# Moving the splitting steps of the next four heads within the attention loop

## The chip, the cores and the metric

The kernel runs on one core of a Trainium2 chip. The metric is the time of one execution on the device in microseconds (us). Three runs of the kernel before took 743.78, 744.02 and 741.24 us, with a median of 743.78 us. The engines are TensorE (PE for its matmuls, PEld for its weight loads), VectorE (DVE), ScalarE (ACT), GpSimd (POOL) and SyncE (SP), which only issues transfers here.

## The reference

An attention in which a query sees only the keys of its own cluster is followed by a mixture of experts: a token goes to one group out of four and in it to one expert out of four.

```python
def _attn_ref(q, k, v, centroids):          # q, k, v: 4 x 8 x 768 x 64
    q_assign = argmax(einsum('bhsd,hcd->bhsc', q_n, c_n), -1)    # 16 clusters a head
    k_assign = argmax(einsum('bhsd,hcd->bhsc', k_n, c_n), -1)
    mask = q_assign[:, :, :, None] == k_assign[:, :, None, :]
    scores = where(mask, scale * matmul(q, k.transpose(0, 1, 3, 2)), -1e9)
    scores = scores - max(scores, -1)
    attn = exp(scores)
    attn = attn / (sum(attn, -1) + 1e-09)
    return matmul(attn, v)
def _moe_ref(x, w_group, w_expert, w1, w2):  # x: 3072 x 512
    ...                                      # group and expert by argmax, softmax weights
    h = maximum(xg[mask_e] @ w1[g, e], 0.0)  # 512 x 1024
    out[tok_idx] = combined[:, None] * (h @ w2[g, e])
```

## The kernel before, in words

The 32 heads of the four batches are worked through one after the other, and each head in nine **units** of 512 columns, so that there are 288 units, numbered g. In each unit TensorE computes a fine score tile `psf` (L421 and L422, from two fp16 halves of each number), a coarse score tile `psc` for a head two heads further on (L379, 18 units ahead), and adds the products with the values of the unit five back to `pso` (L447, L448). ScalarE takes the exponential of `psf` (L426), GpSimd forms the low half of the result (L428), and VectorE takes the row maximum of `psc` (L382). After nine units VectorE and ScalarE divide and store the head's output (`finish`, L461 to L468).

Beside this, the inputs of the heads to come are prepared, four heads (two pairs, p0 and p1) at a time. A group of four heads is called Q and its own units begin at g = 36 Q, so that the preparation has a **cycle of 36 units**; a unit's place in it, g modulo 36, is its phase. The preparation has nine steps, whose units stand in the list `pos`:

- `split` (L199 and `halves`, L223 and L224): the fp16 high half of the keys or queries of a pair is made on ScalarE (L199), and the low half in two pieces, in the step's unit and the next: ScalarE copies half of the input to a `psm` tile (L223) and VectorE subtracts (L224).
- `assign` (L268 to L280): 36 small matmuls give the similarity to the centroids in a `psm` tile, and VectorE turns it into one-hot rows in six instructions (L273, L275, L276, L278, twice L280). Then `spread` sends the halves to their places by transfers on SP.
- `mask` (L336 to L344): the one-hot rows of four heads are transposed, scaled and sent to the score operands. The coarse scores of the group can begin after that, 18 units before its own first unit.
- `splitv` (L249, L223, L224): the same split for the values of a pair, which are needed only five units after the first unit of the pair.

`psm` tiles lie in two PSUM banks that all of these steps share with the transposes of the row maximum (L403), of the routing logits of a finished pair of heads (`logits`, L765 to L779) and of the routing decision of a finished batch (`decide`, L845 to L926). The helper `beside(g)` runs in each unit what `at` has put there, and then at most one of the waiting `turns` (assign, mask, row maximum, logits, routing); a unit in which `halves` took a `psm` tile lets no turn in, and a turn with a lower priority number goes first. A list scheduler then puts each engine's instructions in order and may draw an instruction ahead where its inputs are there: the high half of the values (L249), which needs no `psm` tile, is done some 18 units before the low half.

When the third batch is decided, `first` prepares the first expert beside the last units: it picks the expert, loads and splits its weights (L1042 to L1051), gathers its tokens (L1193) and transposes them to `xTA` (L1208, L1209). After the last unit come the logits and the decision of the last batch, which give the order of the experts (`ei`, L1347) and with it the stream of weights, and beside them the first expert's up-projection (L1236).

The lines that place the nine steps are, for Q from 2 to 7:

```python
g0 = max(0, 9 * (4 * Q - 5) + 1)                       # 36 Q - 44
g1 = 9 * (4 * Q - 2) - 9 if Q > 1 else 15              # 36 Q - 27
pos = [int(g0 + (g1 - g0) * i / (n - 1)) for i in range(n)] if Q > 1 else [...]
at(pos[0], *hold, split, p0, 0); at(pos[1], *hold, split, p0, 1)
at(pos[2], turn, pos[2], assign(p0)); at(max(pos[2], free), spread, p0)
at(pos[6], *((splitv, p0) if Q > 1 else (later, splitv, p0)))
at(pos[8], turn, pos[8], mask(Q))
```

Of the kernel before, what the change touches and what calls it, by code (L numbers as in the profile page):

```python
# [34 lines left out]
def attention(ctx, tc, qT, kT, vr, cen, R, DEN, cfg):  # L35
# [438 lines left out]
    def at(g, f, *a):  # L474
        jobs.setdefault(int(g), []).append((f, a))
# [31 lines left out]

    for Q in range(1, NQ):
        g0 = max(0, 9 * (4 * Q - 5) + 1)
        g1 = 9 * (4 * Q - 2) - 9 if Q > 1 else 15  # L510
        n = 9
        p0, p1 = 2 * Q, 2 * Q + 1
        pos = [int(g0 + (g1 - g0) * i / (n - 1)) for i in range(n)] if Q > 1 else [0, 1, 6, 3, 4, 9, 20, 23, 12]
        hold = (later,) if Q == 2 else ()
        free = max(9 * (4 * Q - 4), 0)
        if Q > 1:
            at(g0 - 4, load, p0)
            at(g0 - 4, loadv, p0)
            at(pos[0], *hold, split, p0, 0)
            at(pos[1], *hold, split, p0, 1)  # L520
        if Q > 1:
            at(pos[0], *((behind, load) if Q == 2 else (load,)), p1)
        at(*((pos[0], loadv) if Q > 1 else (16, behind, loadv)), p1)
        at(pos[2], turn, pos[2], assign(p0))
        at(max(pos[2], free), spread, p0)
        hold = (later,) if Q == 1 else ()
        at(pos[3], *hold, split, p1, 0, Q == 1)
        at(pos[4], *hold, split, p1, 1, Q == 1)
        at(pos[5], turn, pos[5], assign(p1))
        at(max(pos[5], free), spread, p1)  # L530
        at(pos[6], *((splitv, p0) if Q > 1 else (later, splitv, p0)))
        at(pos[7], *((splitv, p1) if Q > 1 else (later, splitv, p1)))
        at(pos[8], turn, pos[8], mask(Q))
# [78 lines left out]
    g, n = 0, AHEAD0  # L612
# [1000 lines left out]
def tile_cluster_attention_moe(ctx, tc, qT, kT, vr, cen, wr, w1, w2, out):  # L1613
# [25 lines left out]
    with ExitStack() as c:  # L1639
        attention(c, tc, qT, kT, vr, cen, R, DEN, cfg)  # L1640
# [58 lines left out]
```

## Time and profile before

| | value |
|---|---|
| median of three runs | 743.78 us |
| the profiled execution, its own time | 742.52 us |
| its span, first to last instruction | 740.7 us |
| PE busy (matmuls) / PEld busy (weight loads) | 720.3 us (97%) / 619.1 us (84%) |
| DVE / ACT / POOL busy | 596.1 / 486.0 / 493.6 us |
| granted TensorE clock, mean of the span | 0.997 |
| units of the attention | about 24 to 402 us of the span |
| experts | about 402 to 740 us of the span |

Busy times are sums over one engine, and engines run beside one another, so that they don't add up to the span. A matmul row is about 0.19 us long, though the next one of the same kind can start 0.03 us later; the matmul row of a short wait can therefore hide part of it. In tables by stretch each engine has its busy time and, in brackets, its number of instructions. "Idle before" in a group is time in which the group's engine had nothing to run just ahead of it, and what ended it stands behind the arrow. The chain of waits goes back from the last instruction and names at each step the work that released the next; a stretch in which the chain stays on one engine is paced by that engine.

### The profile page before, as it was taken

Reading aid. Unit: us, or ns where it says so; the run is one execution under the profiler, and the core shown is the slowest. Engines: PE = TensorE matmul, PEld = TensorE weight load, DVE = VectorE, ACT = ScalarE, POOL = GpSimd, SP = SyncE. Lnnn points to the kernel's source line nnn. Section 1 sums busy time; section 2 is a strip of 40 time slices with the busy share of each in tenths; the row PEclk is TensorE's granted clock in tenths of the full one; section 3 lists DMA queues with packets and bytes.
Section 4 is the critical chain, followed back from the end, with each engine's and each line's share of the span. In section 5 each row is a group of like instructions: output and inputs, shape, how many; then the busy total and the mean of one; then the engine's idle time right before and its main releaser. Section 6 shows DMA issues by size and latency. Waiting matters only on the chain.

```text
span 740.7 us, 26722 instructions
## 1 busy us (share of the span) xinstructions
PE 720.3 (97%) x11106; PEld 619.1 (84%) x11106; DVE 596.1 (80%) x1216; ACT 486.0 (66%) x952; POOL 493.6 (67%) x491
## 2 busy tenths in 40 slices
PE   8899999999999999999999989999999999999996
PEld 4688788888888888888888677888789999999996
DVE  6899889899888997989876476767779889988961
ACT  7778877788778887677977275444454555555642
POOL 8899787777787877878786325354644688554542
PEclk9999999999999999999999999999999999999998
DMA  8955634435245351240521696866777678887921
GB/s 226 224 141 153 192 100 119 155 99 154 81 120 172 95 159 37 67 131 3 178 81 38 234 313 220 273 211 221 237 244 234 230 272 284 284 275 264 281 77 36
DMA packets 45881, 128.04 MB, mean 173 GB/s; under 512 B 7699, under 2 KB 12691, under 8 KB 45752
## 3 DMA queue, kind: packets, MB, share of 16 engines
q1 hardware_dynamic: 40668, 112.64, 49.8%
q0 software_dynamic: 4928, 13.59, 5.1%
q8 instruction: 89, 1.46, 0.8%
q14 instruction: 40, 0.33, 0.1%
q10 hardware_dynamic: 156, 0.03, 0.0%
HBM read 93.41 MB, written 13.65 MB: 145 GB/s over the span
## 4 chain that ended last, share of the span: by engine, by line
PE 67%; DVE 17%; ACT 6%; issue 5%; DMA 2%; POOL 1%; another core or an unknown queue 1%; POOLq 0%; ACTq 0%; DVEq 0%
PE psh L1236 16%; PE psy L1258 12%; DVE mpart L382 7%; PE pso L447 6%; PE psf L421 6%; PE pso L448 5%; PE psf L422 5%; PE psc L379 5%; PE psy L1272 3%; DVE parts L224 2%; ACT p L426 2%; DMA st<-w 2%; PE psm L765 2%; PE psm L1294 1%; PE psm L1208 1%
## 5 line engine op out<-in xcount | busy, mean ns | idle before, releaser
L428 POOL TENSOR_TENSOR pl<-p 128x512 f16<-128x512 f32 x278 | 285.4, 1042 | 75.1 <-ACT p L426 70.6
L382 DVE TENSOR_REDUCE mpart<-psc 128x1 f32<-128x512 f32 (+1 forms) x282 | 190.2, 682 | 28.8 <-PE psc L379 28.4
L426 ACT ACTIVATE p<-psf 128x512 f32<-128x512 f32 x288 | 169.7, 596 | 45.6 <-PE psf L422 40.4
L447 PE MATMUL pso<-V,p 128*128 128x65 f16 x1152 | 160.2, 193 | 0.0
L448 PE MATMUL pso<-V,pl 128*128 128x64 f16 x1152 | 159.9, 193 | 0.0
L447 PE MATMUL pso<-V,pl 128*128 128x65 f16 x1152 | 159.4, 193 | 0.5 <-POOL pl L428 0.5
L448 PE MATMUL pso<-V,p 128*128 128x64 f16 x1152 | 159.3, 193 | 0.0
L421 PE MATMUL psf<-A 82*128 82x384 f16 (+2 forms) x576 | 142.5, 273 | 1.7 <-ACT p L426 1.6
L422 PE MATMUL psf<-B 128*128 128x384 f16 (+2 forms) x576 | 142.7, 273 | 0.0
L448 PEld LDWEIGHTS <-p 128*128 128x128 bf16 x1152 | 112.2, 97 | 22.2
L447 PEld LDWEIGHTS <-p 128*128 128x128 bf16 x1152 | 113.1, 98 | 9.6 <-issue 1.6
L447 PEld LDWEIGHTS <-pl 128*128 128x128 f16 x1152 | 112.5, 98 | 0.6 <-POOL pl L428 0.6
L448 PEld LDWEIGHTS <-pl 128*128 128x128 f16 x1152 | 111.5, 97 | 0.3
L379 PE MATMUL psc<-A 80*128 80x512 f16 (+1 forms) x376 | 106.3, 325 | 1.9 <-DVE mpart L382 1.2
L1239 DVE SCALAR_TENSOR_TENSOR hl<-psh,hh 128x160 f16<-128x160 f32 (+14 forms) x136 | 49.8, 368 | 48.9 <-ACT hh L1238 43.5
L1238 ACT ACTIVATE hh<-psh 128x160 f16<-128x160 f32 (+14 forms) x136 | 45.8, 345 | 59.1 <-PE psh L1236 54.9
L1301 POOL DMA_INDIRECT out_dram<-y,ri x33 | 43.4, 1316 | 52.4 <-ACT y L1300 46.3
L1236 PE MATMUL psh<-xT,wh0a 128*128 128x288 f16 (+7 forms) x512 | 74.6, 255 | 0.0
L1193 POOL DMA_INDIRECT xg<-xbuf,ri x25 | 40.5, 1620 | 43.7 <-PE psm L1208 30.1
L422 PEld LDWEIGHTS <-B 128*128 128x128 f16 x576 | 56.5, 98 | 10.9 <-issue 2.3
L1236 PE MATMUL psh<-xT,wh0b 128*128 128x272 f16 (+6 forms) x448 | 64.7, 253 | 0.0
L1236 PE MATMUL psh<-xT,wl0a 128*128 128x288 f16 (+7 forms) x256 | 64.0, 255 | 0.0
(385 smaller groups left out, 1785.9 us busy)
## 6 DMA issues: line engine op xcount, KB each, us to landing
st<-w SPq DMA_DIRECT2D x128, 512.0 KB
B<-parts SPq DMA_DIRECT2D x60, 192.0 KB
kx<-kT SPq DMA_DIRECT2D x16, 384.0 KB
qx<-qT SPq DMA_DIRECT2D x16, 384.0 KB
vx<-vr SPq DMA_DIRECT2D x16, 384.0 KB
xbuf<-xs SPq DMA_DIRECT2D x4, 1536.0 KB
A<-parts SPq DMA_DIRECT2D x30, 192.0 KB
A<-mk SPq DMA_DIRECT2D x56, 24.0 KB
```

Source lines behind the costliest of these rows:

```text
L379: last["mm"] = nc.tensor.matmul(out=pc[:, off:off + k1 - k0], lhsT=QA[h % 8][0:80, c * P:(c + 1) * P], rhs=KA[h % 8][0:80, k0:k1], start=T ...
L382: nc.vector.tensor_reduce(out=(mp[:, 0, 0:1], mp[:, :, 1], mp[:, 1, 0:1])[i], in_=pc.rearrange("p (a x) -> p a x", a=n), axis=AX.X, op=ALU ...
L421: nc.tensor.matmul(out=o, lhsT=KA[h % 8][0:82, ks], rhs=QA[h % 8][0:82, q0:q1], start=True, stop=False)
L422: nc.tensor.matmul(out=o, lhsT=KBs[h][:, ks], rhs=QBs[h][:, q0:q1], start=False, stop=True)
L426: cfg["exp"] = nc.scalar.activation(out=p32, in_=pf, func=AF.Exp, scale=QK / (SQ * SQ))
L428: lo = (nc.vector if u in (EARLY if h < 2 else DVE_LO[h % 8] if h < NH - 2 else DVE_END) else nc.gpsimd).tensor_tensor(out=pl, in0=p32, in ...
L447: nc.tensor.matmul(out=O[:, col:col + 65], lhsT=p[:, bs], rhs=vh, start=c == 0 and q == 0 and i == 0, stop=False, skip_group_check=True)
L448: nc.tensor.matmul(out=O[:, col:col + 64], lhsT=p[:, bs], rhs=vl, start=False, stop=c == NCH - 1 and i == 1, skip_group_check=True)
L1236: self.mm = nc.tensor.matmul(out=ph[:, 0:M], lhsT=w[:, k, fs], rhs=xT[:, a, k], start=i == 0, stop=i == 3 * KD - 1)
L1238: nc.scalar.activation(out=hh[:, f], in_=ph[:, 0:M], func=AF.Relu)
L1239: self.ev = nc.vector.scalar_tensor_tensor(out=hl[:, f], in0=ph[:, 0:M], scalar=0.0, in1=hh[:, f], op0=ALU.max, op1=ALU.subtract)
L1258: self.mm = nc.tensor.matmul(out=py[:, 0:M], lhsT=w[:, f, d * P:(d + 1) * P], rhs=a[:, f], start=i == 0, stop=i == len(prods) - 1)
```

## The change

Only the units of the nine steps change, for the groups Q = 2 to 7. Written as the number of units ahead of the group's first unit:

| step | before | after |
|---|---|---|
| split p0, keys or queries | 44 and 42 | 44 and 41 |
| assign p0 | 40 | 38 |
| split p1 | 38 and 36 | 36 and 33 |
| assign p1 | 34 | 31 |
| values p0, values p1 | 32 and 30 | 24 and 20 |
| mask | 27 | 27 |

The four splits of keys and queries, which followed one another two units apart, now mostly have three units each, and the values go behind the mask, to phases 12 and 16. The loads of the inputs and the `spread` of p0 keep their units; the `spread` of p1 moves by three.

```diff
     for Q in range(1, NQ):
         g0 = max(0, 9 * (4 * Q - 5) + 1)
-        g1 = 9 * (4 * Q - 2) - 9 if Q > 1 else 15
-        n = 9
         p0, p1 = 2 * Q, 2 * Q + 1
-        pos = [int(g0 + (g1 - g0) * i / (n - 1)) for i in range(n)] if Q > 1 else [0, 1, 6, 3, 4, 9, 20, 23, 12]
+        pos = [36 * Q - x for x in (44, 41, 38, 36, 33, 31, 24, 20, 27)] if Q > 1 else [0, 1, 6, 3, 4, 9, 20, 23, 12]
```

Line numbers behind this place are two lower in the changed kernel.

On VectorE, in the cycle of the group Q = 4, the values of p0 (`V_192`) stand in the block of the preparation before, between the row maxima (L382), the second pair's one-hot rows (L273 to L276) and the end of a head (L461 to L466):

```order
L382 TENSOR_REDUCE mpart_220<-psc 128x1 x2
L224 TENSOR_TENSOR V_192<-psm,V_192 128x6x64
L273 TENSOR_REDUCE mx<-psm 128x24
L224 TENSOR_TENSOR V_192<-psm,V_192 128x6x64
L382 TENSOR_REDUCE mpart_220<-psc 128x2
L461 TENSOR_SCALAR DEN<-pso 128x6
L275 TENSOR_TENSOR psm<-psm,mx 128x384
L463 RECIPROCAL rec<-DEN 128x6
L382 TENSOR_REDUCE mpart_220<-psc 128x1
L466 TENSOR_TENSOR pso<-pso,rec 128x6x64
L276 TENSOR_TENSOR psm<-psm,desc 128x384
```

In the changed kernel the values of both pairs stand behind the block:

```order
L382 TENSOR_REDUCE mpart_218<-psc 128x1
L224 TENSOR_TENSOR V_192<-psm,V_192 128x6x64
L382 TENSOR_REDUCE mpart_218<-psc 128x1
L224 TENSOR_TENSOR V_192<-psm,V_192 128x6x64
L382 TENSOR_REDUCE mpart_218<-psc 128x2
L461 TENSOR_SCALAR DEN<-pso 128x6
L463 RECIPROCAL rec<-DEN 128x6
L466 TENSOR_TENSOR pso<-pso,rec 128x6x64
L382 TENSOR_REDUCE mpart_218<-psc 128x1
L468 TENSOR_TENSOR xs<-pso,xs 128x6x64
L224 TENSOR_TENSOR V_193<-psm,V_193 128x6x64
L382 TENSOR_REDUCE mpart_218<-psc 128x1
```

The four value halves (L224) have moved from among the one-hot rows to a place where the row maxima and the end of a head alone stand beside them.

On ScalarE, around the start of a head (phases 35 to 3), in the cycle of Q = 4 as well, the kernel before has, between the exponentials (L426):

```order
L426 ACTIVATE p_4616<-psf 128x512
L199 ACTIVATE parts<-kx 128x768
L426 ACTIVATE p_4647<-psf 128x512
L426 ACTIVATE p_4690<-psf 128x512
L390 ACTIVATE desc<-m_4670 128x6
L223 ACTIVATE psm<-kx 128x384
L426 ACTIVATE p_4722<-psf 128x512
L406 COPY mr<-psm 6x128
L426 ACTIVATE p_4760<-psf 128x512
L223 ACTIVATE psm<-vx 128x384 x2
```

and the changed kernel:

```order
L426 ACTIVATE p_4612<-psf 128x512
L923 COPY rls<-psm 64x289
L390 ACTIVATE desc<-m_4678 128x6
L426 ACTIVATE p_4655<-psf 128x512
L199 ACTIVATE parts<-qx 128x768
L199 ACTIVATE parts<-kx 128x768
L223 ACTIVATE psm<-qx 128x384
L426 ACTIVATE p_4702<-psf 128x512
L223 ACTIVATE psm<-qx 128x384
L426 ACTIVATE p_4734<-psf 128x512
L406 COPY mr<-psm 6x128
L223 ACTIVATE psm<-kx 128x384
```

The second pair's two high halves (L199) and its first low half now follow one another between two exponentials, and the values' halves (`vx`) are gone from here.

On VectorE at the end of the attention, behind GpSimd's last work that VectorE does for it (L428), the kernel before has the copies of the first expert's transposed tokens (`xTA`) beside the end of the last head (L461 to L468):

```order
L428 TENSOR_TENSOR pl<-p_11278 128x512
L1209 COPY xTA<-psm 128x8x128
L779 TENSOR_TENSOR lg<-psm,lg 128x60
L1209 COPY xTA<-psm 128x8x128
L461 TENSOR_SCALAR DEN<-pso 128x6
L1209 COPY xTA<-psm 128x8x32
L463 RECIPROCAL rec<-DEN 128x6
L466 TENSOR_TENSOR pso<-pso,rec 128x6x64
```

and the changed kernel:

```order
L428 TENSOR_TENSOR pl<-p_11276 128x512
L777 TENSOR_TENSOR lg<-psm,lg 128x60
L1049 TENSOR_TENSOR wl1a<-psm,wh1a 128x2x256
L1207 COPY xTA<-psm 128x8x128
L461 TENSOR_SCALAR DEN<-pso 128x6
L463 RECIPROCAL rec<-DEN 128x6
L466 TENSOR_TENSOR pso<-pso,rec 128x6x64
L1207 COPY xTA<-psm 128x8x128
L468 TENSOR_TENSOR xs<-pso,xs 128x6x64
L1207 COPY xTA<-psm 128x8x32
L1250 MEMSET yh 128x48
L1250 MEMSET yl 128x48
```

The preparation of the first expert has moved some units back: a half of its weights (`wl1a`) and all three copies of `xTA` now stand among the last head's instructions, and the second large copy is ahead of the last head's low half (`xs`).

## Rows read from the trace of the kernel before

**Rows 1.** Busy us by engine (instructions), clock, DMA in each stretch of the span.
```profile
core 0: us, PE busy (x) PEld busy (x) DVE busy (x) ACT busy (x) POOL busy (x), PEclk, DMA share, GB/s
60.00:96.00 36.00, 34.44 (x674) 28.58 (x671) 30.01 (x66) 30.35 (x61) 29.23 (x38) 1.00 0.57 156
96.00:132.00 36.00, 36.00 (x712) 30.05 (x711) 32.27 (x70) 27.77 (x58) 30.21 (x45) 1.00 0.42 118
132.00:155.00 23.00, 22.74 (x447) 19.36 (x445) 19.03 (x49) 18.03 (x37) 17.41 (x17) 1.00 0.36 114
155.00:180.00 25.00, 24.54 (x488) 20.34 (x487) 24.50 (x60) 20.93 (x46) 19.44 (x19) 1.00 0.60 164
180.00:203.00 23.00, 22.85 (x430) 19.36 (x430) 18.22 (x40) 17.93 (x36) 17.39 (x17) 1.00 0.30 82
...
226.00:250.00 24.00, 23.73 (x467) 20.11 (x464) 20.02 (x52) 19.06 (x39) 17.99 (x19) 1.00 0.34 110
250.00:275.00 25.00, 24.38 (x489) 20.26 (x487) 24.50 (x59) 20.69 (x44) 19.35 (x19) 1.00 0.61 165
...
298.00:345.00 47.00, 46.67 (x934) 39.49 (x933) 41.61 (x98) 32.57 (x66) 37.37 (x37) 1.00 0.27 77
345.00:402.00 57.00, 56.22 (x1151) 48.36 (x1148) 45.67 (x106) 48.47 (x98) 43.73 (x42) 1.00 0.26 86
sum 342.00, PE 337.56 PEld 284.57 DVE 294.74 ACT 270.87 POOL 268.92; mean PE 30.69 PEld 25.87 DVE 26.79 ACT 24.62 POOL 24.45
```

**Rows 2.** Waits of TensorE from 60 to 402 us: total us, times, longest us.
```profile
PE psf L421 <- ACT p L426: 1.0, 2, 0.7
PE psm L765 <- DVE oh L280: 0.9, 3, 0.3
PE psc L379 <- DVE mpart L382: 0.8, 2, 0.4
PE psm L922 <- DVE oh L280: 0.6, 2, 0.3
PE psm L403 <- DVE parts L224: 0.4, 1, 0.4
PE psm L403 <- DVE oh L280: 0.4, 2, 0.2
```

**Rows 3.** The chain of waits by line, 155 to 180 us, then 180 to 203 us.
```profile
by line: DVE mpart L382 40.5%; DVE parts L224 15.6%; DVE V L224 6.0%; ACT psm L223 6.0%; DVE oh L280 4.3%; DVE pso L466 4.1%; DVE psm L275 3.8%; DVE psm L276 3.8%; DVE rmv L890 3.7%; DVE mw L278 3.7%; issue 3.3%; DVE xs L468 1.9%; DVE rec L
by line: PE pso L447 17.4%; PE pso L448 17.1%; PE psf L421 16.7%; PE psf L422 16.5%; PE psc L379 16.2%; PE psm L765 6.2%; PE psm L922 4.0%; PE psm L773 3.7%; PE psm L336 1.5%; DVE oh L280 1.2%; PE psm L403 0.5%; issue 0.2%
```

**Rows 4.** Groups of instructions, 60 to 402 us: busy us, mean ns, idle before.
```profile
L224 DVE TENSOR_TENSOR V<-psm,V 128x384 f16<-128x384 f32 x24 | 13.2, 550 | 0.6
...
L223 ACT ACTIVATE psm<-vx 128x384 f32<-128x384 f32 x24 | 11.8, 493 | 4.9 <-DVE V L224 4.9
...
L199 ACT ACTIVATE parts<-qx 128x768 f16<-128x768 f32 x12 | 10.1, 840 | 2.6 <-issue 1.5 <-PE psm L268 1.1
```

**Rows 5.** Timeline of TensorE: start us, us, instruction, idle before.
```profile
171.07 0.22 PE L403 MATMUL psm<-ident,desc 128*128 128x128 f16 x1 [0.18 <-DVE oh L280]
```

**Rows 6.** Timeline of TensorE at the end of the attention.
```profile
402.15 0.36 PE L1208 MATMUL psm<-ident,vx 32*128 32x32 f16 x8
402.89 0.41 PE L1236 MATMUL psh<-xTA,wh 128*128 128x288 f16 x2 [0.38 <-DVE xTA L1209]
```

**Rows 7.** Timeline of VectorE there.
```profile
401.30 0.69 DVE L1209 COPY xTA<-psm 128x1024 f16<-128x1024 f16 x1 [0.73 <-PE psm L1208]
402.25 0.17 DVE L461 TENSOR_SCALAR DEN<-pso 128x6 f32<-128x6 f32 x1 [0.27 <-PE pso L448]
...
402.97 0.57 DVE L466 TENSOR_TENSOR pso<-pso,rec 128x384 f32<-128x384 f32 x1
...
404.13 0.56 DVE L468 TENSOR_TENSOR xs<-pso,xs 128x384 f16<-128x384 f32 x1 [0.26 <-ACT xs L467]
```

**Rows 8.** Busy us by engine behind the handover, as in rows 1.
```profile
416.00:446.00 30.00, 26.91 (x293) 21.75 (x292) 15.36 (x29) 17.24 (x31) 11.14 (x12) 1.00 0.94 323
```

## The prediction

> **What bounds the kernel now.** I read the busy time by stretch first. From 60 to 402 us TensorE's matmuls are busy for 337.56 of 342 us at full clock [rows 1], so that the attention is bound by matmuls which the change doesn't touch, and at most 4.44 us there can be had from it. The same rows say where these lie. The block of the nine steps of Q = 4 falls into 155 to 180 us, that of Q = 6 into 250 to 275 us: there VectorE is busy for 24.50 of 25 us, 98%, and TensorE stands still for 0.46 and 0.62 us, and for 0.15 us behind the first. The stretch behind it, 180 to 203 us, has VectorE at 18.22 of 23 us, 79%. The chain of waits says the same in another way: in the block nearly every step of it is VectorE's, row maxima, low halves and one-hot rows, while behind it nearly every step is a matmul [rows 3]. So in the block VectorE sets the pace, with TensorE kept busy out of what stands ready, and behind it TensorE alone.
>
> The waits of TensorE by name come next [rows 2]. Seven of them, 1.9 us in all, end with the last one-hot instruction of an `assign` (oh L280), which gives a `psm` tile back: three times a routing transpose (L765) waited for that tile, twice the decision (L922), twice a transpose of the maxima (L403). Three of the seven stand alone at the end of the blocks of Q = 3, 5 and 7 and are the whole idle time of 132 to 155 (0.26), 226 to 250 (0.27) and 298 to 345 us (0.33); four stand in the two blocks at 98%. The other waits: one low half (0.4) and one row maximum (about 0.4) in the cycle of Q = 2, before 96 us; one wait of 0.7 for an exponential, in the same cycle; and a row maximum and an exponential beside the first expert's weights, in 345 to 402 us.
>
> A short wait costs more than its print. A matmul row is 0.22 us long [rows 5], but 712 matmuls fill 36.00 us from 96 to 132 us, where nothing is missing, 0.05 us each [rows 1]; a wait that begins inside such a row hides up to 0.17 us more. That is an estimate from the two rows.
>
> **The change, part by part.** *The values leave the block.* Their high halves (L249) were drawn ahead before and stay where they were. What moves is four low halves a cycle: on VectorE 4 x 0.550 = 2.2 us, on ScalarE 4 x 0.493 = 2.0 us [rows 4], six times. No work is removed. The block goes from 24.5 to 22.3 of 25 us on VectorE, 89%; where the values now stand, 18.2 + 2.2 = 20.4 of 23 us is 89% as well. What does 89% cost? From 96 to 132 us VectorE is busy for 32.27 of 36 us, 90%, and TensorE for all 36.00; from 298 to 345 us, 41.61 of 47 or 89%, TensorE lost only the one wait for a `psm` tile [rows 1]. So I put the pace-setting by VectorE at nothing on both sides, covered by TensorE's ready work, and if that cover is gone it costs the 0.46 to 0.62 us that the 98% rows show. ScalarE, which waited 4.9 us for VectorE in the values' steps [rows 4], comes free as well.
>
> For Q = 3 to 7 that gives: the idle time of the two full blocks, 0.46 + 0.15 + 0.62 = 1.23 us, and four hidden ends of 0.17, together 1.9 us, taken whole. The three waits alone at the ends of the other blocks, 0.86 us and three hidden ends, 1.37 us, are a matter of the tile and not of the load: `assign` holds its tile through six VectorE instructions with row maxima in between, which pass a little faster when no value stands among them, but the second `assign` also moves three units closer to the routing. Half, 0.7 us. Sum 2.6 us, bounds 0 and 3.3.
>
> *Q = 2.* From 60 to 96 us TensorE lost 36 - 34.44 = 1.56 us. The two VectorE waits (about 0.4 each, with hidden ends 1.1 us) have the same cause as the full blocks; but inputs come late here, since this group's loads share the transfers with the start. I take half, 0.6 us. The ScalarE wait of 0.7 us stays. Bounds: 1.1 us gained, or 0.7 lost, if the values, now at units 48 to 53, bring a second such wait.
>
> *The keys and queries are spread out.* One free unit behind each pair of units gives turns a place, which is counted above. On ScalarE two high halves (L199, 0.84 us each) and a low half (0.493) now follow one another without an exponential between, 2.17 us against units of about 378 / 288 = 1.31 us. Before, one high half passed an exponential at a time. What this costs is not in the trace: the nearest row is the wait for an exponential of 0.7 us, behind one late high half. In three cycles that would be 0 to 2.1 us. I take nothing, because TensorE has coarse scores, products with the values five units back and transposes to run meanwhile, and because ScalarE is busy only 17 to 21 us of 23 to 25 [rows 1]; the upper end stays for the range. The `spread` of p1 on SP, now 31 units ahead, is needed from the coarse scores on, 18 units ahead. Of what stands in SP's queue with it, the loads of values are nearest to the moved steps: the next pair's load (L87) is put 12 units ahead of the group, eight behind the last values, so that it waits for nothing new. GpSimd gets and loses nothing.
>
> *The end of the attention.* The steps of Q = 7 and the turns behind them come later, and with them the first expert. Before, the last head's products ended at 402.25 us, when the last copy of `xTA` but one had been made at 401.30, and the first up-projection began at 402.89 [rows 6, 7]. Afterwards VectorE has, by the new order, the quotient (to 402.97 + 0.57 = 403.5), a copy of `xTA` (0.69, to 404.2), the last head's low half (0.56, to 404.8) and the small copy (0.29, to 405.1). That is 2.2 us later, in which TensorE can do the 12 transposes of the last head, 12 x 0.05 = 0.6 us, that came after before. So 1.6 us idle. Behind it, from 416 to 446 us, TensorE has 3.09 us of waits with the DMA engines at 94% [rows 8]: the stream of weights sets the pace there, and its start hangs on the decision, not on `xTA`. A delay ahead of such waits can vanish in them. I take half, 0.8 us; bounds 0 and 2.2. The idle time of 345 to 402 us (0.78 us) only moves with the first expert's weights: 0.
>
> Sum: 2.6 + 0.6 - 0.8 = 2.4 us. The profiled execution of 742.52 us would come to 740.1, and the median of 743.78 us, which is 1.26 above it, to **741.4**.
>
> **Rivals.** *The tile, not the load (743.9).* Seven waits are for a `psm` tile and the change adds none. Each step still takes tiles from the same two banks, so a wait that leaves the block may turn up where the values now stand, among the maxima and routing. Only the two L403 waits in the full blocks would go, 2 x (0.18 + 0.17) = 0.7 us [rows 5], and the end of the attention takes its 0.8 back: 743.9. For it: three of the seven stand in stretches at 83 to 89%, with no full VectorE [rows 1, 2]. Against it: the two full blocks lost 1.23 us, the light stretches 0.3 each. The Trainium skill (Perfetto Trace Analysis, Identifying Performance Opportunities, Optimization Strategy) says that the same gap repeating on the engine that should be saturated can mean too little SBUF or PSUM for the next tile. By that page this rival is the likelier; the repeated wait behind L280 agrees with it, the 98% of VectorE in two blocks doesn't.
>
> *Nearly everything goes (738.6).* If the even load removes all waits but those of the first expert, 4.44 - 0.78 = 3.66 us with nine hidden ends of 0.17, 5.2 us in all, and the later start of the first expert vanishes in the waits for weights: 738.6. For it: 36.00 of 36 us at 90%. Against it: the waits for the tile, and Q = 2 with its late inputs.
>
> *Slower (746.0).* One mechanism at one place: the first expert's up-projection behind VectorE's four instructions after the last product. If it starts the whole 2.2 us later, the weights' waits absorb none of it and the waits in the blocks only move, the kernel takes 743.78 + 2.2 = 746.0. It decides as soon as the delay that is left at 446 us is above what the blocks gave, at 0.7 us with the tile rival. For it: between 402 and 446 us no other work is ready in amount. Against it: 3.09 us of waits stand behind it.
>
> That the change doesn't do what it says is true in part: the high halves of the values stay, and half of ScalarE's share with them. It is in the sum.
>
> **How the numbers follow.** Chances: forecast 0.42 (its own range 739.8 to 743.2), nearly everything 0.25, tile 0.22, slower 0.11. About 0.5%, 3.7 us, is what a measurement of this kernel can tell from no change: below 740.06 or above 747.5 us. Below lie most of "nearly everything" (0.22) and the lower end of the forecast (0.06), 0.28; above, the upper end of "slower", in which waits for exponentials come on top, 0.04; 0.68 between. The range from 738.0 to 745.3 leaves out the lower end of the one (0.05) and most of the slower case (0.09).
>
> **What would show it.** Right: VectorE near 89% in the block of Q = 4 and of Q = 6 and behind it; the chain there passing to matmuls; fewer waits of L765, L922 and L403 for L280; idle time in both full blocks near zero. Wrong: the same waits 10 to 20 units later, or exponentials (L421 waiting for p) at phases 35 to 3 in the cycles of Q = 4 and 6. For the end: the first up-projection less than 1.5 us or more than 2.5 us behind the last product plus the 0.6 that it had before, and the waits of 416 to 446 us falling by as much or not. A change of over 0.5% in either direction with the attention's idle time unchanged would make the whole reading wrong.

## The result: slower, in three places

The changed kernel took 751.83 us (median of six runs), the kernel before 743.16 us beside it: a ratio of 1.0125, with an interval from 1.0110 to 1.0139. The forecast was 741.4 us with a range of 738.0 to 745.3, so that sign and range were both wrong. The profiled execution took 751.07 us, its span is 749.0 us, 8.3 more than the 740.7 before.

Where the 8.3 us arise is read from five marks in the two traces: the exponential (L426) of unit 284, the first instruction of the last head's end (DEN, L461), the last matmul of the first expert's up-projection, the first transposes of the next tokens (`xg`), and the end.

| from, to | before | after | difference |
|---|---|---|---|
| start to unit 284 | 395.18 | 396.58 | +1.4 |
| unit 284 to DEN | 7.07 | 8.42 | +1.35 |
| DEN to the last matmul of the up-projection | 16.13 | 17.48 | +1.35 |
| from there to the transposes of `xg` | 10.80 | 14.83 | +4.0 |
| from there to the end | 311.5 | 311.7 | +0.2 |

The same stretches of the changed kernel as in [rows 1], with the same columns:

```profile
60.00:96.00 36.00, 34.80 (x674) 28.80 (x671) 30.58 (x67) 29.59 (x60) 29.24 (x38) 1.00 0.51 133
96.00:132.00 36.00, 35.38 (x712) 29.76 (x709) 30.89 (x65) 27.00 (x55) 29.34 (x44) 1.00 0.45 126
...
155.00:180.00 25.00, 24.53 (x493) 20.58 (x492) 24.36 (x62) 20.48 (x43) 18.64 (x19) 1.00 0.52 144
180.00:203.00 23.00, 22.80 (x437) 19.23 (x436) 18.79 (x42) 18.92 (x37) 18.17 (x19) 1.00 0.34 89
203.00:226.00 23.00, 22.35 (x456) 18.69 (x455) 19.22 (x42) 16.30 (x33) 17.64 (x18) 1.00 0.42 112
...
250.00:275.00 25.00, 24.35 (x493) 20.45 (x490) 24.18 (x62) 20.41 (x45) 18.79 (x19) 1.00 0.47 134
...
sum 342.00, PE 336.39 PEld 282.56 DVE 292.13 ACT 267.22 POOL 266.90; mean PE 30.58 PEld 25.69 DVE 26.56 ACT 24.29 POOL 24.26
```

TensorE stands still for 342 - 336.39 = 5.6 us, 1.2 more than before. In the two full blocks its idle time is what it was, 0.47 and 0.65 us, and there is new idle time where the kernel before had none: 0.62 us in 96 to 132 us, and 0.65 in 203 to 226 us, where the row of the kernel before is

```profile
203.00:226.00 23.00, 23.00 (x469) 19.25 (x468) 20.70 (x44) 17.31 (x36) 19.13 (x20) 1.00 0.49 134
```

By its length the attention loses in the cycles of Q = 3 and Q = 5. From the exponential of unit 64 to that of unit 100 the five profiles with the changed attention (named below) take 47.9 to 48.6 us, from unit 136 to 172 48.6 to 49.4 us, where the four with the old attention take 47.4 us in both; in the cycle of Q = 4 (100 to 136) they take 46.8 to 47.1 us against 47.3.

VectorE is not at 89% in the two full blocks but at 97% (24.36 and 24.18 of 25 us). The values did go: in the window of the block of Q = 4 the kernel before has three of their four halves, the changed one has all four behind it. VectorE's groups of `V`, 155 to 180 us before and 180 to 203 us after:

```profile
L224 DVE TENSOR_TENSOR V<-psm,V 128x384 f16<-128x384 f32 x3 | 1.7, 551 | 0.1
```

```profile
L224 DVE TENSOR_TENSOR V<-psm,V 128x384 f16<-128x384 f32 x4 | 2.2, 553 | 1.1 <-ACT psm L223 1.1
```

But their time in the block was filled again, by row maxima and routing that had stood elsewhere: VectorE executed 62 instructions there instead of 60. This stretch, which one engine paces, didn't get lighter by the work that was taken out; it took in the next work.

The waits of TensorE from 60 to 402 us in the changed kernel, to be held against [rows 2] (total us, times, longest us):

```profile
PE psm L403 <- DVE parts L224: 1.9, 4, 0.6
PE psf L421 <- ACT p L426: 1.8, 6, 0.7
PE psc L379 <- DVE mpart L382: 0.4, 2, 0.2
PE psm L763 <- DVE parts L224: 0.4, 1, 0.4
```

All seven waits for the one-hot rows (L280) are gone, as forecast. In their place the transpose of the maxima waits four times for a tile that a low half of keys or queries (L224) holds, and the fine scores wait six times for an exponential. ScalarE, just before the second of the four:

```profile
169.82 0.84 ACT L199 ACTIVATE parts<-qx 128x768 f16<-128x768 f32 x1
170.57 0.83 ACT L199 ACTIVATE parts<-kx 128x768 f16<-128x768 f32 x1
171.31 0.47 ACT L223 ACTIVATE psm<-qx 128x384 f32<-128x384 f32 x1
171.72 0.57 ACT L426 ACTIVATE p<-psf 128x512 f32<-128x512 f32 x1
```

and TensorE behind it:

```profile
172.43 0.22 PE L403 MATMUL psm<-ident,desc 128*128 128x128 f16 x1 [0.40 <-DVE parts L224]
```

Ahead of it stands the lump of two high halves and a low half for which the prediction took nothing.

The handover on VectorE and on TensorE:

```profile
405.00 0.15 DVE L461 TENSOR_SCALAR DEN<-pso 128x6 f32<-128x6 f32 x1
...
405.89 0.68 DVE L1207 COPY xTA<-psm 128x1024 f16<-128x1024 f16 x1
406.58 0.56 DVE L468 TENSOR_TENSOR xs<-pso,xs 128x384 f16<-128x384 f32 x1
407.06 0.28 DVE L1207 COPY xTA<-psm 128x256 f16<-128x256 f16 x1
```

```profile
407.77 0.41 PE L1234 MATMUL psh<-xTA,wh 128*128 128x288 f16 x2
```

The up-projection begins 2.77 us behind DEN instead of 0.64 [rows 6, 7], 2.1 us later; the prediction had 2.2. What it had not is what came behind. ScalarE, TensorE and GpSimd (the first and the last of these rows of TensorE also bound the fourth line of the table):

```profile
421.33 0.41 ACT L1236 ACTIVATE hh<-psh 128x288 f16<-128x288 f32 x1 [1.06 <-issue]
427.43 0.41 ACT L1236 ACTIVATE hh<-psh 128x288 f16<-128x288 f32 x1 [5.68 <-remote]
```

```profile
422.48 0.29 PE L1234 MATMUL psh<-xTA,wl 128*128 128x288 f16 x1
422.60 1.02 PE L1256 MATMUL psy<-hh,wh1a 128*128 128x288 f16 x7
427.89 0.40 PE L1256 MATMUL psy<-hh,wh1a 128*128 128x288 f16 x1 [4.26 <-ACT hh L1236]
428.08 2.13 PE L1256 MATMUL psy<-hh,wl1a 128*128 128x288 f16 x8
...
437.31 0.61 PE L1206 MATMUL psm<-ident,xg 128*128 128x128 f16 x8
```

```profile
425.05 0.95 POOL L1191 DMA_INDIRECT xg<-xbuf,ri  x1 [0.30 <-issue]
```

The matmul on which the last `hh` waits ends at 422.48 + 0.29 = 422.77 us; ScalarE has nothing else to do, and starts at 427.43 (`remote`: the profile has the release but no instruction for it; that the instruction needs the matmul alone is read from the program). I call these 4.7 us **the pause**. TensorE has seven matmuls to run in it and stands for 4.26 us; then eight matmuls take 2.13 us that take 1.14 before and later. In the trace of the kernel before (its transposes of `xg` for the table's fourth line included) the pause is there too, but behind the last `hh` at 418.70, in front of the first `yh`, and TensorE had 48 matmuls to run through it:

```profile
418.50 1.14 PE L1258 MATMUL psy<-hh,wh1a 128*128 128x288 f16 x8
...
420.46 1.14 PE L1258 MATMUL psy<-hl,wh1a 128*128 128x288 f16 x8
...
429.18 0.61 PE L1208 MATMUL psm<-ident,xg 128*128 128x128 f16 x8
```

```profile
425.29 0.80 ACT L1261 ACTIVATE yh<-psy 128x288 f16<-128x288 f32 x2 [6.17 <-remote]
```

The 24 matmuls on which `yh` waits end at 420.46 + 1.14 = 421.60 us, so that 3.7 of the 6.17 us of ScalarE are the pause; where there is none it waits 2.5 us for these matmuls (after_plain, below). The prediction put the idle time of 416 to 446 us down to the stream of weights.

### The profile page after: what moved, and what is told of

It is laid out like the page before. It is cut to its first block, busy times and chain, and to the rows that moved or that the text cites. A ratio compares the mean times of both kernels' runs of the same rounds, so it can differ in the third digit from the quotient of the medians.

```text
span 749.0 us, 26734 instructions
## 1 busy us (share of the span) xinstructions
PE 722.0 (96%) x11106; PEld 620.0 (83%) x11106; DVE 601.5 (80%) x1216; ACT 485.0 (65%) x952; POOL 493.4 (66%) x491
## 4 chain that ended last, share of the span: by engine, by line
PE 64%; DVE 13%; issue 7%; ACT 7%; DMA 5%; POOL 1%; another core or an unknown queue 1%; SPq 1%; POOLq 0%; ACTq 0%; DVEq 0%
PE psh L1234 14%; PE psy L1256 11%; PE psf L421 6%; PE pso L447 6%; PE psf L422 6%; PE pso L448 6%; PE psc L379 5%; DVE mpart L382 4%; PE psy L1270 3%; DMA B<-parts 3%; ACT p L426 2%; DMA st<-w 1%; PE psm L268 1%; ACT parts L199 1%; PE psm L1292 1%
## 5 line engine op out<-in xcount | busy, mean ns | idle before, releaser
L428 POOL TENSOR_TENSOR pl<-p 128x512 f16<-128x512 f32 x278 | 285.8, 1041 | 78.2 <-ACT p L426 72.8
L382 DVE TENSOR_REDUCE mpart<-psc 128x1 f32<-128x512 f32 (+1 forms) x282 | 190.6, 682 | 26.6 <-PE psc L379 25.8
L426 ACT ACTIVATE p<-psf 128x512 f32<-128x512 f32 x288 | 169.4, 594 | 50.3 <-PE psf L422 45.8
L421 PE MATMUL psf<-A 82*128 82x384 f16 (+2 forms) x576 | 142.4, 273 | 2.7 <-ACT p L426 2.2
L1191 POOL DMA_INDIRECT xg<-xbuf,ri x25 | 38.6, 1543 | 44.8 <-PE psm L1206 32.0
L421 PEld LDWEIGHTS <-A 82*128 82x128 f16 x576 | 55.7, 98 | 10.6 <-issue 2.6
```

What stands on the lines that cost most here:

```text
L382: nc.vector.tensor_reduce(out=(mp[:, 0, 0:1], mp[:, :, 1], mp[:, 1, 0:1])[i], in_=pc.rearrange("p (a x) -> p a x", a=n), axis=AX.X, op=ALU ...
L421: nc.tensor.matmul(out=o, lhsT=KA[h % 8][0:82, ks], rhs=QA[h % 8][0:82, q0:q1], start=True, stop=False)
L426: cfg["exp"] = nc.scalar.activation(out=p32, in_=pf, func=AF.Exp, scale=QK / (SQ * SQ))
L428: lo = (nc.vector if u in (EARLY if h < 2 else DVE_LO[h % 8] if h < NH - 2 else DVE_END) else nc.gpsimd).tensor_tensor(out=pl, in0=p32, in ...
```

## The experiments

All of them are the changed kernel with other numbers in `pos`, unless said otherwise; before2, after2 and after3 are the two kernels unaltered. A ratio is against the kernel before, timed beside it. "Attention" is the time from the exponential of unit 28 to that of unit 284; four profiles of the kernel before or with its attention give 332.3 to 333.2 us, five with the changed attention 333.1 to 335.8, mean 334.8. "Handover" is DEN to the first matmul of the up-projection, "behind" the last matmul of the up-projection to the transposes of `xg`, from start to start.

| run | ratio | attention | handover | behind |
|---|---|---|---|---|
| values_only | 1.0020 (1.0001 to 1.0039) | 330.6 | 2.76 | 8.95 |
| steps_only | 1.0205 (1.0166 to 1.0244) | 346.6 | 0.64 | 8.94 |
| not_last | 1.0032 (1.0011 to 1.0053) | 335.1 | 0.64 | 8.95 |
| only_last | 1.0044 (1.0030 to 1.0059) | 333.2 | 2.77 | 8.94 |
| before2 | 1.0014 (0.9997 to 1.0030) | 332.3 | 0.64 | 10.65 |
| after2 | 1.0071 (1.0046 to 1.0096) | 333.1 | 2.76 | 10.42 |
| p1_at_37 | 1.0076 (1.0047 to 1.0105) | 333.4 | 2.77 | 11.09 |
| values_not_last | 1.0002 (0.9990 to 1.0014) | 331.2 | 0.64 | 10.71 |
| after3 | 1.0096 (1.0080 to 1.0113) | 335.6 | 2.76 | 11.97 |
| after_slots_later | 1.0096 (1.0081 to 1.0111) | 335.8 | 2.76 | 9.85 |
| before_slots_later | 1.0017 (1.0004 to 1.0029) | 332.6 | 0.63 | 9.93 |
| after_plain | 1.0059 (1.0045 to 1.0073) | 335.2 | 2.77 | 8.95 |
| p0_new | 1.0039 (1.0023 to 1.0054) | 334.9 | 0.64 | 10.82 |
| p1_new | 1.0024 (1.0012 to 1.0035) | 334.1 | 0.63 | 10.79 |
| q7_values_old | 1.0048 (1.0030 to 1.0066) | 337.0 | 0.64 | 10.83 |
| before_plain | 0.9981 (0.9967 to 0.9995) | 332.4 | 0.64 | 8.95 |
| values_not_last2 | 1.0002 (0.9991 to 1.0012) | 331.5 | 0.64 | 10.71 |
| values_psy3 | 0.9981 (0.9971 to 0.9991) | 331.8 | 0.63 | 9.45 |

**The parts of the change (four runs on one chip).** My theory after the result was that all the loss begins with the values of the last group.

```diff
-(44, 41, 38, 36, 33, 31, 24, 20, 27)
+(44, 42, 40, 38, 36, 34, 24, 20, 27)                        # values_only
+(44, 41, 38, 36, 33, 31, 32, 30, 27)                        # steps_only
+(44, 41, ..., 20, 27) if Q < 7 else (44, 42, ..., 30, 27)   # not_last
+(44, 41, ..., 20, 27) if Q == 7 else (44, 42, ..., 30, 27)  # only_last
```

> Only the values move (24 and 20 units ahead of the group), the other steps keep the places of the kernel before. Theory of the end: the 8.3 us that the changed kernel's profiled span is longer (749.0 against 740.7) arise behind 396 us, and begin with the values of the last group, whose four pieces in units 228 to 233 keep turns out and so put the first expert's preparation back. Then this kernel has nearly the whole loss: 749.5 to 752.5 us, the first up-projection (L1234) starts about 2 to 3 us behind the end of the last products (L461's DEN instruction) instead of 0.6, and ScalarE's last hh (L1236) stands alone behind a wait of 5 to 6 us. Rival, the splits: the new waits of L403 for low halves of keys and queries (1.9 us in the changed kernel) and what follows from them are the loss: 743 to 746 us here.

> Only the seven other steps move, the values stay 32 and 30 units ahead. Theory of the end: no loss of more than about 1 to 2 us, 743 to 746, with the first up-projection 0.6 us behind the last DEN as before, though waits of L403 for parts L224 may be there (1 to 2 us in all). Rival, the splits: 748 to 752 us.

> The change for the groups Q = 2 to 6 alone; the last group, Q = 7, keeps the old places. Theory of the end: the handover is that of the kernel before, 743 to 746 us; the attention's own share of the loss, if any, is what is left (0 to 2.5 us). Rival, the loss gathers over all cycles: 5/6 of it here, 749 to 751 us.

> The change for the last group, Q = 7, alone. Theory of the end: nearly the whole loss, 749 to 752 us, with a 4 us wait of L1256 for ACT hh and the lower clock behind it. Rival, the loss gathers over all cycles: 1/6 of it, about 744.5 us.

Both theories missed in the times; of the first one the handovers came as expected. The values alone lost 0.2%, not the whole; their attention is 2 us shorter, as forecast for the whole change, and their handover 2.1 us longer. The steps alone lost 2%, in every cycle, and not at the handover: there the second pair's pieces (33, 32), its `assign` (31) and the values (32 to 29) want the same units, and the row maxima come too late. Three of TensorE's waits in steps_only, from 60 to 415 us:

```profile
PE psf L421 <- DMA A<-mr: 3.0, 4, 1.1
PE psc L379 <- DVE mpart L382: 3.0, 6, 0.6
PE psm L403 <- ACT mk L339: 1.8, 2, 1.0
```

So the values had to leave if the steps were to be spread, and the loss has two roots: the five cycles without the last (+0.32%, all of it in the attention) and the last cycle alone (+0.44%, 2.1 us at the handover and 1.1 between unit 284 and DEN). In none of these four profiles was there a pause ("behind" 8.95 us, the matmuls' own time); the kernel before took 738.93 us beside them, and 741.9 to 742.4 beside the later ones.

**The same kernels again, a gap, and the values without the last group.**

```diff
-(44, 41, 38, 36, 33, 31, 24, 20, 27)
+(44, 41, 38, 37, 33, 31, 24, 20, 27)                        # p1_at_37
+(44, 42, 40, 38, 36, 34, 24, 20, 27) if Q < 7 else (44, 42, ..., 30, 27)  # values_not_last
```

> The kernel before once more, for its profile on the chip of these four runs: with the four runs ahead of this one the kernel before took 738.93 us, against 743.16 beside the changed kernel, and their traces have no pause between a matmul's end and the engine that waits for it where the two first traces have one (ScalarE's 6.17 us ahead of yh). Theory of the pause: a span below 738 us goes with ScalarE's yh (L1261) about 3 us behind its last hh, a span of 740 us or more with 6 to 7 us. Rival, the difference lies all over the kernel: then the attention's end (DEN) and the part behind xg shorten as well.

> The changed kernel once more, on the same chip as the others here. Theory of the parts: the attention ends some 2 to 3 us later than before and the first up-projection starts 2.1 us later behind it than before, together about 4 us of span; only where the pause behind the start of the weights' stream falls on the last hh (L1236 late by 4 us or more) do 4 us come on top. So without the pause 3 to 5 us slower than the kernel before, with it 8 to 9. Rival, the pause belongs to the change: 8 to 9 us slower here too.

> The changed kernel with one number altered: the first split of the second pair 37 instead of 36 units ahead, so that a free unit lies between its second piece (36) and the unit 34 ahead, where the maxima's transpose (L403) is due. Theory of the late half: the four waits of L403 for parts L224 at phases 1 and 2 (0.5 to 0.75 us each) shrink to a third, and the attention ends 1 to 2 us sooner than in the changed kernel. Rival, the tile: the wait only passes to another user of the tile and the attention ends within 0.5 us of the changed kernel.

> Only the values move, and only for Q = 2 to 6; the last group keeps all its old places. Theory: the attention is shorter by 1 to 2 us, as in the run with the values alone (unit 270 at 379.9 against 381.3 us), and the handover is that of the kernel before, 0.6 us from the last DEN to the first up-projection: 1 to 2 us faster than the kernel before. Rival: what the attention gains is given back at its end, same time within 0.7 us.

before2 has the pause again (6.03 us ahead of `yh`, a span of 740.5 us), as its theory said. The changed kernel took from 743.1 to 753.2 us in single runs here, the kernel before 740.1 to 745.3; by the profiles it is what lies behind the start of the stream that varies ("behind" is 14.83, 10.42 and 11.97 us in after, after2 and after3). p1_at_37 took the waits of L403 for low halves away entirely, and the time stayed (747.49 against 747.46 us), as the rival said: the same tile is waited for by others now. Its first four waits for a `psm` tile, of 3.8 us in all where the changed kernel has 2.5:

```profile
PE psm L336 <- ACT xTr L766: 1.6, 2, 1.0
...
PE psm L336 <- DVE oh L280: 0.7, 1, 0.7
PE psm L403 <- DVE lg L775: 0.5, 1, 0.5
PE psm L763 <- DVE parts L224: 0.4, 1, 0.4
```

values_not_last has the shorter attention and the old handover, and yet the time of the kernel before.

**The pause.** In after_slots_later and before_slots_later the lookup and its six gathers stand behind the up-projection. In after_plain and before_plain the first four gathers are plain transfers, which read rows without an index (they leave out the choice of those tokens).

```diff
-    X.slots()
     for i, _ in enumerate(ga):
+        if i == 7:
+            X.slots()
```

```diff
-        self.got = nc.gpsimd.indirect_dma_start(out=xg[0:n]..., in_offset=..., **src)
+        self.got = nc.gpsimd.dma_start(out=xg[0:n]..., in_=R.xbuf[0:n])
```

> The changed kernel again, as the reference on the chip of these four runs. In two jobs it took 8.7 us more than the kernel before (750.7 to 754.4) and 5.5 us more (743.1 to 754.7, scattered), so the part behind the start of the weights' stream seems to change from run to run. Theory of the parts: 4 us fixed (attention's end and handover), and 0 to 6 us that vary, in which the last hh (L1236) waits. So 743 to 755 in single runs, the profile's hh late by as much as its span is above the others. Rival, a fixed loss: all runs within 1.5 us of each other.

> The changed kernel with the lookup of the next tokens and its six gathers behind the first expert's up-projection instead of in its midst (gathers about 5 us later; nothing else moves). Theory of the gathers: the pause begins some 4 to 5 us after the first gather, so that the last hh comes through on time (within 0.5 us of its last matmul) in all runs; 4 to 6 us faster than the changed kernel where that is at its slow end, and little scatter. Rival, the weights' stream: the pause lies 5 to 10 us behind the first load of weights whatever the gathers do; the last hh waits as before and the time is that of the changed kernel.

> The kernel before with the same move (gathers about 3 us later). There the last hh is through before the pause, and the first yh (L1261) waits in it. Theory of the gathers: the pause moves back by 3 us with the gathers and catches yh as before: same time within 1.5 us, or 1 to 3 us faster where the pause gets shorter. Theory of the stream: pause unchanged, and the next transposes wait for the later tokens: 0 to 2 us slower.

> The changed kernel, where the first four of the six gathers (the rows of one tile and of the first rank's tokens) are plain transfers of as many rows from the start of the same table, on the same engine's queue: no index, other rows. Leaves out the choice of these tokens. Theory of the gathers by index: no pause, hh on time, 744 us or less. Rival, the stream: the pause stays. Third, any transfer that GpSimd starts there does it: pause stays, too, and only the run with the later gathers tells.

The four runs of after3 lie within 1.7 us, nearer to its rival than to its theory. The pause goes with the gathers. With the later gathers the last `hh` is on time, and the pause stands in front of the second `yh`, again 1.5 us behind the end of the last gather; the time is the same, since the wait only moved. before_slots_later does likewise: its first `yh` is on time, its second waits 5.72 us, until 1.5 us behind the last gather. ScalarE and GpSimd in after_slots_later:

```profile
423.44 0.41 ACT L1236 ACTIVATE hh<-psh 128x288 f16<-128x288 f32 x1 [1.06 <-PE psh L1234]
427.17 0.41 ACT L1259 ACTIVATE yh<-psy 128x288 f16<-128x288 f32 x1 [3.32 <-PE psy L1256]
433.04 0.41 ACT L1259 ACTIVATE yh<-psy 128x288 f16<-128x288 f32 x1 [5.46 <-PE psy L1256]
```

```profile
430.60 0.94 POOL L1191 DMA_INDIRECT xg<-xbuf,ri  x1 [0.30 <-issue]
```

With four gathers made plain there is none: `hh` follows its matmul, and `yh` 2.9 us later the 24 matmuls of its group. ScalarE in after_plain (three lines lower in its code):

```profile
423.38 0.41 ACT L1239 ACTIVATE hh<-psh 128x288 f16<-128x288 f32 x1 [1.06 <-PE psh L1237]
426.32 0.41 ACT L1262 ACTIVATE yh<-psy 128x288 f16<-128x288 f32 x1 [2.53 <-PE psy L1259]
```

That is 746.56 us against the 749.85 of the changed kernel beside it. But the plain transfers didn't run where the gathers had run. They need no index, and GpSimd was through with them 5 us before SP issued the first weights of the stream (418.47 us); the two gathers by index that are left were through at 421.65 us. GpSimd in after_plain:

```profile
410.98 1.73 POOL L1192 DMA_DIRECT2D xg<-xbuf  x3
412.70 0.54 POOL L1192 DMA_DIRECT2D xs<-xbuf  x1
419.35 1.03 POOL L1194 DMA_INDIRECT xg<-xbuf,ri  x1 [6.11 <-DVE rg L1317]
420.68 0.97 POOL L1194 DMA_INDIRECT xg<-xbuf,ri  x1 [0.30 <-issue]
```

So with six gathers beside the stream there was a pause in these runs, and with two there was none. Whether the index, the number of the gathers or the place beside the stream decides is not shown, and the third theory, any transfer of GpSimd there, wasn't tested. Of the theories of the slots one half was right: the pause goes with the gathers, but to move them only moves it.

**What was still open: which pair, which group, and what the pause costs before.**

```diff
-(44, 41, 38, 36, 33, 31, 24, 20, 27)
+(44, 41, 38, 38, 36, 34, 24, 20, 27)   # p0_new, Q < 7; Q = 7 as before
+(44, 42, 40, 36, 33, 31, 24, 20, 27)   # p1_new, Q < 7; Q = 7 as before
+(44, 41, 38, 36, 33, 31, 32, 30, 27)   # q7_values_old, Q = 7; Q < 7 as changed
```

> For Q = 2 to 6 the values at the new places and, of the steps, only the first pair's (44 and 41, assign 38); the second pair's steps as before (38 and 36, assign 34); Q = 7 as before. Theory of the second pair: its first split at 36 brings both high halves and a low half together on ScalarE and a late half ahead of the maxima's transpose, so this kernel is free of that: unit 270 within 1 us of the run with the values alone for these groups, same time as the kernel before within 1 us. Rival, the first pair: 2 us slower than the kernel before.

> As before this one, but with the second pair's steps new (36 and 33, assign 31) and the first pair's old (44 and 42, assign 40). Theory of the second pair: L403 waits for parts L224 at phases 1 and 2 and L421 for exponentials, 2 to 3 us in all, and the time is 2 us or more above the kernel before. Rival: same time as the kernel before.

> The changed kernel, in which only the values of the last group stand 32 and 30 units ahead as before. Theory of the turns: the routing decision of the third batch is taken in unit 238 again instead of 242, the first expert is ready in time, and the first up-projection starts 0.6 us behind the last DEN instead of 2.8; about 744 to 746 us, the collision of values and splits in one cycle included. Rival, the steps of the last group: the handover stays late, 748 us or more.

> The kernel before, where the first four of the six gathers behind the decision are plain transfers of as many rows from the start of the table, as in the run of the changed kernel with plain transfers. Leaves out the choice of these tokens. Theory of the pause: the kernel before, too, loses time in it, though less: 1.5 to 3.5 us faster than the kernel before (739 to 740.5 where that takes 742), yh 3 us behind the last hh. Then the change costs 6 to 7.5 us without any pause. Rival: its pause is covered, same time within 1 us.

It is not the second pair alone. Beside the values' new places, the first pair's steps cost 3.6 us of attention, the second pair's 2.9, both 3.8 (335.1 and 331.2 us). These are single profiles, and the five of the changed attention differ by 2.7 us; the times agree in kind (+0.39, +0.24 and +0.32% against +0.02%), though not_last is from the runs without a pause. ScalarE's lump, which only the second pair's places should bring, is at most a part. In each run others wait for the tile, in p0_new

```profile
PE psm L268 <- ACT mr L406: 1.4, 4, 0.4
PE psm L771 <- DVE slots L924: 0.9, 2, 0.4
```

and in p1_new

```profile
PE psm L763 <- DVE lg L775: 2.2, 3, 0.9
PE psm L763 <- DVE lg L777: 0.8, 2, 0.4
```

q7_values_old settles the handover: with the last group's values at their old places it is 0.64 us again, though the group's other steps are the new ones. Their four pieces keep turns out of units 228, 229, 232 and 233, where the routing of the third batch has its turns; the decision (L865 of the kernel before) comes in unit 242 instead of 238 and the first expert's token lists (L1109) in 268 instead of 264, as the order of the two programs and the traces show; in q7_values_old both are back at 238 and 264. The time stays at 746.59 us: the cycle of units 208 to 244, where values and splits now stand together, takes 48.6 us instead of 47.0. before_plain says that the kernel before, too, loses 1.35 us (0.2%) in the pause.

**A version from this.** values_psy3 is values_not_last with three banks for the down-projection's results, so that TensorE has a third group of products to run in the pause, and two instead of three for the expert stage's `psm`.

```diff
-tc.tile_pool(name="ps_y", bufs=2, space=PSUM)
+tc.tile_pool(name="ps_y", bufs=3, space=PSUM)
-tc.tile_pool(name="ps_m2", bufs=3, space=PSUM)
+tc.tile_pool(name="ps_m2", bufs=2, space=PSUM)
```

> Again the values alone at the new places, for Q = 2 to 6. Theory: the attention from unit 28 to 284 takes 331 us against 332.3 to 333.2 in the profiles of the kernel before; 0 to 1.5 us faster. Rival: its gain is scatter of single profiles: same time within 0.5 us and 332 us or more here.

> The same, with three PSUM banks instead of two for the results of the down-projection (psy) and two instead of three for the tiles (psm) of the expert stage. Theory of the cover: TensorE runs the third group of products in the pause, and the transposes of the next tokens (L1206) come 9 us behind the last up-projection instead of 10.7: 1 to 2 us faster than the run beside it, unless the tile taken away costs as much in the experts. Rival: the pause holds TensorE for another reason: no gain, or slower by the missing tile.

It took 740.53 us against 741.87 of the kernel before and 741.95 of values_not_last2: the pause costs what its cover lacks, and this version beats the kernel before by 0.2% (0.9971 to 0.9991). Its "behind" is 9.45 us, not 8.95; in the third group TensorE still stands for 0.35 us at 423.82 us. The tile that was taken away is missed later, in a wait of 1.0 us of L1204 at 438.08 us. The values alone were no faster in either timing, although the attention of the four profiles with them alone is 0.8 to 2 us shorter than the mean of the kernel before; where that time goes is open.

## Why the prediction was wrong

Two terms turned the sign: the spread keys and queries, put at nothing, and the delay at the end, of which half was to vanish in the waits behind it. The gain of 1.9 us from the full blocks' idle time failed as well.

- **The block lightened by 2.2 us of VectorE, its idle time taken whole: wrong.** Three of the four halves, 1.7 us, had stood in that window; they left, but the block stayed at 97% and kept its idle time (0.47 and 0.65 us). The error was to take the row at 90% for the block's future: it belonged to a stretch that has less to do. What the values gave is in the length: 46.6 us in the cycle of Q = 4 where they alone moved, against 47.3.
- **The seven waits for L280, 1.9 us: they went, as forecast, and the time didn't follow.** The values alone gave 0.8 to 2 us of attention, against 2.6 forecast for Q = 3 to 7, and nothing of it showed in the time.
- **"The keys and queries are spread out: I take nothing": the first term that turned the sign.** It measured about 3.5 us for Q = 2 to 6 (335.1 for not_last against 331.2 to 331.8 in the three profiles with the values alone there), above the bound of 2.1. Against those three profiles, TensorE's waits of two kinds are longer in the five of the change (60 to 402 us): for an exponential 1.0 to 2.9 us instead of 0.5 to 0.9, for a `psm` tile 2.2 to 2.5 instead of 1.6. The prediction had seen the first and put it at nothing, because TensorE had other work meanwhile; the second it had not priced. Which of the two costs more, and why it falls on the cycles of Q = 3 and Q = 5, stays open: the first pair's steps, which bring no such lump, cost nearly as much alone.
- **"The tile, not the load" was the better rival, but not the whole.** Waits for a `psm` tile were 2.2 to 2.7 us in the four profiles before, 2.2 to 2.5 in the five of the change, and 3.7 to 4.2 in p1_at_37, p0_new and p1_new, mostly at other lines: they move, as this rival said. They don't measure the loss, since p1_at_37 with 3.8 us of them has 333.4 us of attention and the change with 2.5 has 334.7. The Trainium skill's sentence on repeated gaps (Perfetto Trace Analysis, Identifying Performance Opportunities, Optimization Strategy) pointed to the tiles, and waits for them are there in every placement. Whether a third buffer for `psm` in the attention would end them wasn't tried.
- **The end of the attention: right in size, wrong in its place.** 2.1 us later behind DEN, where 2.2 was forecast. But DEN itself came 1.35 us later in the last units, because the first expert's preparation ran into them (its transposes, L1206, wait there for 0.60 us behind the logits' `lg`, and L421 for 0.31 us for an exponential); the prediction had counted only what stood behind the last product.
- **"A delay ahead of such waits can vanish in them. I take half": wrong, and the largest term.** The waits of 416 to 446 us were for the larger part not the stream's but the pause's (10.80 us "behind" instead of 8.95, 1.85 of 3.09; values_only and not_last, without a pause, have 0.75 us of idle time there), and a delay doesn't vanish in it but brings its own last step, the eighth `hh`, into it: 4.0 us in the profiled execution. In the runs with plain transfers the change costs 0.59 + 0.19 = 0.8%, or 5.8 us by the two profiled spans (743.7 and 737.9); the rest of the 8.7 us, about 3, is the pause, an estimate, since these runs and the first ones were not taken together.
- The slower rival named the right mechanism for a part, 2.1 us of 8.3, and got 0.11; a loss of over 0.5% got 0.04. Each loss was bounded alone and none was added to another.

## What to carry to other kernels

Work taken out of a stretch that one engine paces need not show as idle time there: here it was filled from behind; its gain must be looked for in the length of the whole loop. Where many steps share two buffers in turns, a moved step can move the wait to the next user of the buffer, so price a move by the whole sequence of takers, and follow it to the work whose turns come last. And before idle time is counted as a cushion, find out what ends it: ask which work would stand there if everything ahead came two microseconds later.

## What the runs showed of the hardware

While GpSimd's gathers by index ran beside the stream of weights, an engine that needed a matmul's result could start up to 4.7 us after the matmul's end: 427.43 against 422.77 us. In eleven of the fourteen profiles with a pause it ended 1.4 to 1.6 us behind the end of the last gather (425.05 + 0.95 = 426.00 in the changed kernel). In the other three, all with the late handover, it ended elsewhere: 1.5 and 0.9 us before that end in after2 and p1_at_37, and with it in after3. With two of the six gathers beside the stream there was none. Why the four runs beside a kernel before of 738.93 us had no pause with the same six gathers, and by what way the gathers hold the signal up, stays open.

After the 4.26 us without matmuls TensorE ran at a lower clock. Stretches of the changed kernel, columns as in [rows 1], the granted clock behind the brackets:

```profile
422.60:427.90 5.30, 1.04 (x10) 0.69 (x8) 0.03 (x1) 0.41 (x1) 2.78 (x3) 0.96 1.00 355
427.90:431.50 3.60, 3.60 (x18) 2.36 (x18) 0.43 (x1) 0.00 (x0) 0.00 (x0) 0.58 1.03 372
431.50:440.00 8.50, 8.50 (x76) 6.87 (x75) 4.96 (x7) 5.01 (x7) 0.95 (x1) 1.00 0.25 77
```

0.58 is close to the lower of its two levels, 1.2 of 2.4 GHz, for most of 3.6 us; the eight matmuls of 2.13 us and those behind them (to 431.43, 3.35 us for sixteen against 1.96 before) cost 1.4 us.
